# Four of ten turned x tiles change their copying engine, and a written order of pieces is revised

## The chip, the cores and the metric

The kernel runs on one core of a Trainium2 chip, as one program with one launch. The time is device microseconds of that core. Before the change the median of three runs is 315.41 us (315.05 to 315.96). TensorE multiplies matrices, VectorE and ScalarE do elementwise work, GpSimd does elementwise work and issues the loads, SyncE issues the stores. Each of them works through its own queue in order and waits for the others by semaphores.

## The reference

Two computations follow each other. The first is an attention over 8 batches of 8 heads with 576 positions of 64 values, where a position looks back at most 127 positions and a bias falls off linearly with the distance:

```
scores = scale * np.matmul(q, k.transpose(0, 1, 3, 2))
bias = slopes[:, None, None] * (-np.abs(rel).astype(np.float32))[None, :, :]
mask = (rel >= 0) & (rel < window)
scores = np.where(mask, scores + bias[None], -1000000000.0)
attn = np.exp(scores - max) ; attn = attn / (sum + 1e-09)
x = np.matmul(attn, v), rows (batch, position), columns (head, value)
```

The second is a two-layer network on these 4608 rows of 512 columns:

```
h = x @ w_in                      # 512 -> 2048
g = np.where(h > 0.0, h, np.exp(np.minimum(h, 0.0)) - 1.0)
out = g @ w_out                   # 2048 -> 512
```

Inputs and output are float32; the kernel multiplies in float16.

## The kernel before

Both parts run interleaved, so that TensorE always has matmuls of one part while the other waits. Attention works by batch and by blocks of 128 positions: four whole ones and one of 64 in each batch (i = 0 to 4). For a block, TensorE makes the scores, ScalarE exponentiates them into the tiles EX, and VectorE multiplies these with a table of bias and mask (`weigh`, line 234). TensorE multiplies with the values (`values`, `all_values`), and VectorE takes the reciprocal of the row sums and normalises the result into a tile xn of 128 rows and 512 columns.

The network needs x with columns on the partitions. `turn_x` transposes an xn tile on TensorE, four matmuls into one PSUM bank, and one instruction (line 287) then copies that bank into the buffer xT, as float16. Which engine copies is an argument of `turn_x`, called `copy`. In batches 2 to 7 the bank is always `sp[3]`, the second half of the PSUM pair `spb`, which the scores and the last block's values use too.

The hidden layer runs in 144 steps (`hidden`). A step multiplies a part of `w_in` with columns of xT into one PSUM bank of 512 columns. From step 18 on the two banks `hp0` and `hp1` alternate, so a step can begin only when the bank of the step two before it is free again. To free it takes three instructions in a row: an exponential on ScalarE (line 313) and a clamp on GpSimd (line 315), or, for steps in the set SOFT, a Relu and an exponential on ScalarE (lines 309 and 311); and then the ELU on VectorE (line 323), which reads the bank and writes g. Earlier steps use three or more banks.

The output layer, beyond its first 256 rows, is done by Strassen's scheme on blocks of 128 rows and 256 columns: sums and differences of g blocks on VectorE (`sums`, line 354), 896 single products on TensorE (`product`, line 393), copies out of PSUM on ScalarE (`keep`, lines 400 and 402), combinations on VectorE and the stores.

The order of all this is written out in the kernel. The kernel builds one list for each kind of piece: f and b, i, j for the first two batches' turns, biases, scores and exponentials; v, r, n for values, reciprocal and normalising; t for the transposes of an x tile and tA or tD for its copy; h for a hidden step, p and q for its two activations (or the activation and the clamp), e for its ELU; o for one product, u, s1 to s4, c1 to c3 and m for what belongs to the output; k, x, y, w for later scores, their exponentials and the weighing; d for the turning of q and k of later batches; l for loads; a and C for tables. The string `SCRIPT` then names the kinds one after the other, and each name emits the next piece of its list; `o4` emits four products. An engine's queue is thus the SCRIPT cut down to the pieces of that engine. Within a kind the order can't change. tA is the name of the copy list whatever engine does the copy.

PSUM is tracked by tile: an instruction that writes one half of the pair `spa` or `spb` waits for those that still read the other half.

Of the kernel before, what the change touches and what calls it, by code (L numbers as in the profile page):

```python
# [18 lines left out]
def kernel(  # L19
# [58 lines left out]
    sp = [t[:, i, :] for t in (spa, spb) for i in range(2)]  # L78
# [9 lines left out]
    s1 = one([128, 2 * H * 6 * D], F16, "s1")  # L88
# [62 lines left out]
    with tc.manual_schedule():  # L151
# [127 lines left out]
        def turn_x(b, i, copy, bank, c0=0):  # L279
            n = 128 if i < 4 else 64  # L280
            o = (b * S + 128 * i) % RING
            x = xnt.pop((b, i)).rearrange("p g h d -> p (g h d)")
            t = bank.bitcast(F16)[:, c0:c0 + 512].rearrange("p (c r) -> p c r", c=4)
            for c in range(4):
                nc.tensor.transpose(t[:, c, 0:n], x[0:n, 128 * c:128 * c + 128], ident[0:n, 0:n])  # L285
            yield
            copy(xT[:, :, o:o + n], t[:, :, 0:n])  # L287
# [239 lines left out]
        SOFT = {15 + 8 * n + d for n in range(2, 2 * NTB) for d in (0, 1, 2, 3, 4, 7)} | set(range(11, 19)) | {20, 22, 23} | set(range(16 * NTB - 10, 16 * NTB + 8))  # L527

        SCRIPT = """
            f f fD b fD f f fA b fD i C C C i j b C i j v v b r j n r j n t j tD v v r  # L530
            h r n n p t f tD q fA
            h e i f j f fD f fA b fD p b q i i l e j
            h b p
            h j q j l
            h e p v q p i r l n v j
            h r n q e t l p b e i q tD
            h j l e v p
            h r n q v p v e
            h q r
            h p a e q O p n q  # L540
            h r e l n t p O a tA e q v
            h l r e
            h l p a l q O p l e
            h q l
            h e p n l q O p e l
            h q l e t O l tA p a l
            h a q l a f p l f O1 fD l
            h fA O2 l e O p l s3 q O s1 l q e f l f e fA f fD l f O fA fA l a o1 i O1 i a l j o1 O2 o3 s2 o2 l o2 j o2 W o3 j o2 i u i W j v o2 c1 o1 v o1 r o2 r j o1 n i n j o2 W o2 u o1 t o1 s4 o1 tA o1 v o2 j r
            h W n v W p o1 i r
            h q j d n l e o1 v p o1 t W o1  # L550
            h q tA r u l e o2 p o1 v d o1 i r q n
            h j n l e o1 t p W o2
            h u q d tA l o1 e o1 p i d v j q
            h d l e o2 p o1 r o2 W o1
            h q n l e o1 v p o2 r o1 v n q u
            h r c2 l e v p t l n o3 tA r o2 s1 o2 q l k n e o1 x
            h s2 y o2 w
            h p w o4 u o2 s3 q v o3 p e t o3 q o1 c1 o1
            h tA e u o1 r o1 p
            h n q d o3 c3 p t o1 e o1 m tA o4 s4 o1 u k q d  # L560
            h x e o2 p o1 w o2
            h y q d l o1 e o2 u o2 p o2 w o3
            h q c2 l e v p d o1
            h l r q n l o1 e o1 p o1 t o1 l o1 s1 tA o5 q l s3 k u e l
            h x s2 o2 p
            h w u s4 q o4 p o1 e o4 y o2 c1 o3 c3 o1
            h q m w o1 e o1 v u p o2 r
            h n q d o2 p t o2 e o1 tA o3 u k d q
            h e x d o2 p o3 w o2 u
            h q y l e o4 p o1 w o1  # L570
            h q d o1 l v p e v l o1 c2 q o3 r o1 r
            h l e n l v p o3 r o1 n o1
            h q n s1 u o2 p o1 e t o2 tA o1 c3 o3 s2 q k m u
            h e x s3 o2 p o2 w
            h q c1 o1 y o1 e o8 p o1 w o1 t o1 q
            h u e tA o2 p o1 v o1
            h r q n u o1 s4 o1 p o1 t o2 e tA o1 q o4 u k l e
            h x d o2 p o1 w o4 y
            h q c2 l e o2 p o3 w o2 l
            h q u e l o2 p v s1 l  # L580
            h q r l n o2 p o2 e o2 k u s2 q
            h x e o1 c3 o2 p o2 m o2
            h q c1 y e o5 w o2 p o2
            h w q o2 e p t o2 v u s3 q o3 r
            h tA n u s4 o2 p o1 t e o2 tA o1 q o4 u k l e d
            h x c3 o1
            h p w y q s3 o4 l o1 e o2 p o4 c2 l o2 q
            h w l e o2 p v l s1 o1
            h q l r s2 u o1 e m o1 p o1 v o1 n v q o3
            h r r e o1 n o1 p o2 n o2  # L590
            h u d q c1 t o1 s4 o1 tA o4 e o1 p t o2 tA o1 q k u
            h e x d o1
            h p d q o4 p o1 e o4 y o1 q o1 w o2
            h u w u o2 p o1 e v o3 q o1 r
            h n l e o2 p t l o2 s1 o1 tA o4 q c2 k l u e
            h x l d o2 p
            h s2 l q l o3 p o1 e o4 y o2 w o1
            h q w o2 u o1 v e p o2 r o1 q
            h n c1 o2 e p t o3 tA o1 c3 o3 s3 q m k u e
            h x s4 o2 p o1 w o4 u o1  # L600
            h q y e o6
            h p w u q o1 v p l e o5 r q o1
            h n l e t o1 l o1 c3 tA o3 s3 o2 p l k c2 u q l d m
            h x l e o3 s1 l o1 p o3
            h w q y o1 e o7 p o1
            h w u s2 q v p c1 o2 e v q o4 r o1 r v e o1
            h u n
            h r p n n q o3 t o1 e o1 tA o5 p s4 o1 t u
            h d tA q k p e o1 x o1 q o1 d o3
            h e y w o4 p o2 w o1  # L610
            h u q l o1 e o1 p o2 v
            h q r l n o1 c2 o1 l p o1 t e o2 tA o2 s3 o1 l o1 u k q s1
            h l x e o1 c3 o1 p o2 s2
            h m u q w o2 p o1 e o4 y o2 c1 o5
            h q w o1 e v u p o2 r
            h n q d o2 p t o2 e o1 tA o4 q s4 k u e
            h x o1
            h p w y q o4 l o1 e o2 p o4 w u o1
            h q l e o1 v p c2 l
            h r q n l o2 d p o2 l o1 t o1 e o1 tA o1 l o4 u s1 o1 q k l s3 l o1 x o1 s2  # L620
            h e u o2 p o1 s4 o5 q w o3
            h y c1 e o3 p o1 w o2
            h q v e p o1 v c3 u o2 q r v m r o1 n
            h r n o2 n p o3 e o2 u t o1 d o1 tA o1
            h q t e o2 tA o2 p k q
            h x e o2 p o3
            h u c2 q y l o1 e o4 p o2 w o2 l o1
            h q w u l e o1 v p o2 r o2 l o1 n q
            h u e l t p o2 s1 o3 tA
            h s2 q o1 c3 k p e m o1 x o1 s3 o6 s4 o1  # L630
            h q c1 y e o5 w o1 p o3
            h w q u v e p o2 r o1 u o1
            h n q d t o2 tA o1 e o3 p k d u q
            h x e o2 p o2 w
            h y q o2 e o1 p o4 w o2 q o1
            h c2 u e v p o2 r
            h q n s3 o3 t s1 o2 tA o4 e o1 p k u s2 q o2 d
            h x e o2 p o2 c3 o3 c1 o1 m q o1
            h w y e o4 s4 o1 p o3
            h w q u v e p v r v r o2 n o1 u o3 q  # L640
            h r n n o1 e o1 p o1 t o2 tA
            h q u e t o2 tA o2 p k q
            h x e o2 p o2 c2 o3 w o1 q o3
            h y e o1 s1 o2 p o3 w
            h q u o1 e v p o3 r o1 u
            h n q s2 o1 t p o2 e o2 tA o3 c1 o1 q k s3
            h x e s4 o2 p o1
            h w u q c3 o3 p m o1 e o4 y o7
            h q w u e v o2 r o1 u
            h n p t q o2 tA o3 e o2 p k c2 q  # L650
            h x e o2 p o1 w o5 q o3
            h y e o1 s1 o2 p
            h w u q o1 s2 o1 v u p e o6 q r o1
            h c1 n o2 p o1 e o2 k q c3 s3 m o1 x
            h e o1 y o1 w o5 s4 o2 p
            h w u q o1 t o1 p o1 e o3 v u q o2
            h tA e r o2 p o1 n o3
            h u q e v p v o4 q
            h c2 r e o2 p o1 n o5 q
            h u e o2 p o2 r o1 s1 o3 q o1  # L660
            h n u e t p o1 s2 o5 q
            h tA e o2 p o2 c1 t s3
            h q e o2 p o3 s4 o2 tA o1
            h q c3 u m e o2 p o5
            h q u e o2 p o5
            h q u e o2 p o5
            h q c2 e o2 p o4 s1 o1
            h q u e o2 p o3 s2 o2
            h q e o2 p o3 s3 o3 q
            h u e o2 p o2 s4 o1  # L670
            h q c1 o1 e o1 p o6 q
            h u e o2 p o2 c3 o3
            h m q u e o2 p o5 s3 o1 q
            h u e o2 p o3 s1 o1 P q c2 s2 o2 U o1 e o4 P u s1 s2 c4 P c1 s4 P U P U P U c4 c2 Z
        """

# [11 lines left out]
        def parts(f, *kinds):  # L688
            for x in kinds:
                job(x, next, f, None)  # L690
# [87 lines left out]
        n = 2 * NTB - 1  # L778
# [50 lines left out]
```

## Time and profile before

| what | value |
|---|---|
| median of 3 runs | 315.41 us (315.05 to 315.96) |
| the profiled execution | 315.81 us |
| its span, first to last instruction | 314.0 us |
| granted TensorE clock | 0.999 |
| x tile copies on ScalarE (line 287) | 37, of which 34 from `spb` |
| x tile copies on VectorE (line 287) | 3 |
| ELU on VectorE (line 323), 128x512 from the banks hp | 138, mean 682 ns |
| clamp on GpSimd (line 315) | 44, mean 663 ns |

The page gives busy time by engine and the chain of work that ended last, followed back from the end. The timeline gives instructions in order of time: start, duration, engine, line, operation, tiles written <- tiles read, shape, count, and in brackets the idle time ahead of it and what ended that. A row of the copy line gives the count, and the shortest, median and longest duration in ns. Rows of idle time are read as: who ended the wait, microseconds, times.

### The profile page before, as it was taken

What the parts mean: (1) busy time and instruction counts of PE and PEld (TensorE: products, weight loads), DVE (VectorE), ACT (ScalarE), POOL (GpSimd) and SP (SyncE); (2) the same over time, 40 slices, a digit from 0 to 9 for tenths busy, and PEclk for the clock granted to TensorE, in tenths of its full rate; (3) what the DMA queues carried; (4) which work ended last, traced back from release to release, by engine and by line L of the source; (5) the groups of instructions that cost most, each with busy time, mean ns of one, the idle gap of its engine ahead of it and who ended that gap; (6) DMA issues with size and microseconds to landing.
All of it is one profiled execution on the core that took longest, in us unless ns stands there. A gap on an engine that the chain in (4) does not pass through costs nothing.

```text
span 314.0 us, 10000 instructions
## 1 busy us (share of the span) xinstructions
PE 306.1 (97%) x4198; PEld 262.3 (84%) x4198; DVE 257.0 (82%) x499; ACT 250.8 (80%) x452; POOL 109.3 (35%) x163
## 2 busy tenths in 40 slices
PE   8899999999999999999999999999999999999995
PEld 6688876889888889888888888888899888898884
DVE  5658698989999888898889897969988787876773
ACT  4576778869897989878978898879988888868871
POOL 8947857570616052424343152506000001010000
PEclk9999999999999999999999999999999999999999
DMA  9999999987794839290929091939100000000113
GB/s 103 192 194 206 198 160 196 117 83 88 88 114 43 121 53 114 21 161 4 128 55 177 5 135 16 155 60 109 39 35 35 35 33 35 35 37 34 46 58 102
DMA packets 81870, 28.44 MB, mean 91 GB/s; under 512 B 68896, under 2 KB 77728, under 8 KB 81824
## 3 DMA queue, kind: packets, MB, share of 16 engines
q0 software_dynamic: 75920, 18.36, 63.8%
q1 hardware_dynamic: 5760, 9.37, 8.3%
q8 instruction: 33, 0.54, 0.7%
q14 instruction: 13, 0.11, 0.1%
q10 hardware_dynamic: 144, 0.07, 0.1%
HBM read 36.70 MB, written 9.44 MB: 147 GB/s over the span
## 4 chain that ended last, share of the span: by engine, by line
PE 87%; POOL 3%; DVE 3%; DMA 2%; ACT 2%; issue 1%; POOLq 0%; DVEq 0%
PE hp L302 37%; PE op L393 14%; PE av L393 13%; PE spa L223 3%; PE spa L267 3%; DMA VP<-in_v_dram 2%; PE spb L285 2%; PE spb L393 2%; PE spb L302 1%; PE spb L246 1%; DVE g L323 1%; POOL e L315 1%; PE spb L223 1%; PE op L329 1%; PE spa L329 1%
## 5 line engine op out<-in xcount | busy, mean ns | idle before, releaser
L302 PE MATMUL hp<-xT,wi 128*128 128x256 f16 (+3 forms) x1488 | 143.6, 245 | 0.7 <-DVE g L323 0.4
L302 PEld LDWEIGHTS <-wi 128*128 128x128 f16 x1600 | 119.7, 98 | 15.8 <-issue 4.8
L323 DVE SCALAR_TENSOR_TENSOR g<-e,hp 128x512 f16<-128x512 f32 x138 | 94.1, 682 | 31.2 <-ACT e L311 15.5
L315 POOL TENSOR_SCALAR e<-e 128x512 f32<-128x512 f32 x44 | 29.2, 663 | 161.2 <-ACT e L313 158.5
L309 ACT ACTIVATE e<-hp 128x512 f32<-128x512 f32 x98 | 58.7, 599 | 21.5 <-PE hp L302 17.6
L311 ACT ACTIVATE e<-e 128x512 f32<-128x512 f32 x100 | 63.5, 636 | 1.9
L393 PEld LDWEIGHTS <-S 128*128 128x128 f16 x544 | 50.1, 98 | 6.5 <-issue 1.3
L393 PEld LDWEIGHTS <-g 128*128 128x128 f16 x400 | 37.3, 98 | 5.1 <-issue 1.1
L234 DVE TENSOR_TENSOR EX<-EX,TAB 128x1024 f16<-128x1024 f16 x48 | 32.8, 690 | 3.0 <-ACT EX L229 2.5
L115 POOL DMA_DIRECT2D VP<-in_v_dram x40 | 34.4, 870 | 1.4 <-DMA s<-in_k_dram 0.6
L313 ACT ACTIVATE e<-hp 128x512 f32<-128x512 f32 x40 | 24.0, 600 | 7.6 <-PE hp L302 6.9
L393 PE MATMUL op<-T,S 128*128 128x256 f16 x192 | 30.0, 273 | 0.0
L393 PE MATMUL av<-T,S 128*128 128x256 f16 x176 | 27.6, 273 | 0.0
L229 ACT ACTIVATE EX<-spa 128x1024 f16<-128x1024 f32 x24 | 24.6, 1026 | 1.9 <-PE spa L223 1.6
L229 ACT ACTIVATE EX<-spb 128x1024 f16<-128x1024 f32 x24 | 24.4, 1017 | 0.0
L354 DVE TENSOR_TENSOR S<-g 128x1024 f16<-128x1024 f16 (+2 forms) x35 | 22.9, 667 | 0.3 <-PE op L393 0.2
L287 ACT COPY xT<-spb 128x512 f16<-128x512 f16 (+1 forms) x34 | 18.2, 535 | 6.1 <-PE spb L285 5.7
L393 PE MATMUL op<-wo,g 128*128 128x256 f16 x128 | 20.2, 273 | 0.0
L393 PE MATMUL av<-wo,g 128*128 128x256 f16 x120 | 18.3, 273 | 0.0
L109 POOL DMA_DIRECT2D st<-in_k_dram x24 | 16.2, 685 | 3.0 <-DMA s<-in_q_dram 1.9
L275 DVE TENSOR_TENSOR xn<-spa,rden 128x512 f16<-128x512 f32 x24 | 16.5, 687 | 0.6
L109 POOL DMA_DIRECT2D st<-in_q_dram x24 | 15.9, 667 | 0.7 <-DMA VP<-in_v_dram 0.6
(137 smaller groups left out, 419.3 us busy)
## 6 DMA issues: line engine op xcount, KB each, us to landing
out_dram<-ob SPq DMA_DIRECT2D x32, 256.0 KB, 3.2
VP<-in_v_dram POOLq DMA_DIRECT2D x32, 128.0 KB, 5.9
st<-in_k_dram POOLq DMA_DIRECT2D x24, 144.0 KB, 4.5
st<-in_q_dram POOLq DMA_DIRECT2D x24, 144.0 KB, 5.9
wi<-in_moe_w_in_dram POOLq DMA_DIRECT2D x4, 512.0 KB, 11.6
wo<-in_moe_w_out_dram POOLq DMA_DIRECT2D x4, 512.0 KB, 9.7
out_dram<-ob SPq DMA_DIRECT2D x7, 128.0 KB, 1.7
VP<-in_v_dram POOLq DMA_DIRECT2D x8, 64.0 KB, 6.0
```

What stands on the lines that cost most here:

```text
L109: nc.gpsimd.dma_start(st[b][32 * g:32 * g + 32, w, :, :, :, :].rearrange("p h n j d -> p (h n) (j d)"), (q, k)[w][b, 2 * g:2 * g + 2, :, : ...
L115: nc.gpsimd.dma_start(VP[b % 2][0:p, n, :, 0:D], v[b, :, 128 * n:128 * n + p, :].rearrange("h p d -> p h d"))
L229: nc.scalar.activation(unit(b, u)[:, g:g + 2, :, :], (spa, spb)[g // 2].rearrange("p g (h c) -> p g h c", h=2), AF.Exp, scale=0.125)
L234: V.tensor_tensor(out=e, in0=e, in1=TAB[:, int(u == 3), 2 * gp:2 * gp + 2, :, :], op=ALU.mult)
L302: nc.tensor.matmul(p[:, l * w + u0:l * w + u1], w_in_sb[:, c, fc * 128:(fc + 1) * 128], xT[:, c, x0:x0 + u1 - u0], start=(c == 0), stop=(c ...
L309: nc.scalar.activation(e[:, 0:n], p[:, 0:n], AF.Relu, scale=-1.0)
L311: nc.scalar.activation(e[:, 0:n], e[:, 0:n], AF.Exp, scale=-1.0)
L313: nc.scalar.activation(e[:, 0:n], p[:, 0:n], AF.Exp)
L315: nc.gpsimd.tensor_scalar(out=e[:, 0:n], in0=e[:, 0:n], scalar1=1.0, scalar2=0.0, op0=ALU.min, op1=ALU.max)
L323: V.scalar_tensor_tensor(out=gs[t][:, f0:f0 + nf, c0:c0 + w], in0=sh(es.pop((t, c0, f0))), scalar=1.0, in1=sh(hps.pop((t, c0, f0))), op0=A ...
L354: V.tensor_tensor(out=o, in0=a, in1=b, op=op)
L393: nc.tensor.matmul(o, a[:, j, :], b[:, j, :], start=j == 0 and i in (1, 2, 5), stop=j == 7, skip_group_check=True)
```

## The change

In batches 2 to 7 the copies of blocks i = 1 and i = 3 go to VectorE, those of i = 0, 2 and 4 stay on ScalarE. These are 12 of 30 copies, each of 128 partitions and 512 elements. They stay in the list tA.

```
-            parts(turn_x(b, i, copies[0], sp[3]), "t", "tA")
+            parts(turn_x(b, i, copies[i % 2], sp[3]), "t", "tA")
```

(`copies` is `nc.scalar.copy, V.tensor_copy`.) With it, SCRIPT is written anew. It holds the same pieces, each kind as often as before, and many stand a little earlier or later against the hidden steps, mostly by one step, some by up to five. The beginning, a part of the middle and the end:

```
-            f f fD b fD f f fA b fD i C C C i j b C i j v v b r j n r j n t j tD v v r
-            h r n n p t f tD q fA
-            h e i f j f fD f fA b fD p b q i i l e j
+            f f fD b fD f f fA b fD i C C C i j b C i j v v b r j n r j n t j tD v v r f r n
+            h fA n t p i tD j q
+            h e f f fD f fA b fD p b q i i l e j
...
-            h q n d o2 p t o2 e o1 tA o3 u k d q
-            h e x d o2 p o3 w o2 u
-            h q y l e o4 p o1 w o1
-            h q d o1 l v p e v l o1 c2 q o3 r o1 r
+            h n d o2 p t o1 e o2 tA o2 k d q u e
+            h x d o2 p o1 w o2
+            h y q d l o2 e o1 u o2 p o2 w o3
+            h q c2 l e o2 p o1 v l s1 v q o1
...
-            h x c3 o1
-            h p w y q s3 o4 l o1 e o2 p o4 c2 l o2 q
+            h x l e o2 p o1 w o4 y
+            h q c2 l e o2 p o3 w l o3 q o2 c3 o1 l
...
             h u e o2 p o3 s1 o1 P q c2 s2 o2 U o1 e o4 P u s1 s2 c4 P c1 s4 P U P U P U c4 c2 Z
```

More of the change, by code (lines that the diff above doesn't have):

```diff
@@ L529 @@
         SCRIPT = """
-            f f fD b fD f f fA b fD i C C C i j b C i j v v b r j n r j n t j tD v v r
-            h r n n p t f tD q fA
-            h e i f j f fD f fA b fD p b q i i l e j
[L533 to L536, printed above, removed]
-            h j l e v p
[L538 to L568, printed above, removed]
-            h e x d o2 p o3 w o2 u
-            h q y l e o4 p o1 w o1
-            h q d o1 l v p e v l o1 c2 q o3 r o1 r
[L572 to L585, printed above, removed]
-            h x c3 o1
-            h p w y q s3 o4 l o1 e o2 p o4 c2 l o2 q
-            h w l e o2 p v l s1 o1
@@ L589 @@
[L589 to L644, printed above, removed]
+            f f fD b fD f f fA b fD i C C C i j b C i j v v b r j n r j n t j tD v v r f r n
+            h fA n t p i tD j q
+            h e f f fD f fA b fD p b q i i l e j
+            h j
+            h p b j q i p l e
@@ new lines @@
+            h j q v p v l r
+            h r n q n b e p l t e i q
+            h j l e v p
+            h tD r n q v p
+            h r e q v n p
+            h e q r t n p O e tA q
+            h l e
+            h p q v p
+            h l e O r p l n a q
+            h l e l t a O tA p a l
+            h q a q l O e p l e q O l a O1
+            h a O2 l e l f p f fD l q
+            h l e O l p s3
+            h q l fA e l f s1 l p f fA f fD f l O fA q l a O e l o1 i O1 a i j o1 O2 o1 l s2 o6 l j o2 W o3 j o1 i i fA W u v j o2 r o2 c1 v o2 r o1 j o1 n i n j o2 W o1 t o2 tA o1 s4 o3 v j W
@@ new lines @@
+            h r u W v p o3 n i q r o1 d
+            h j l n e o1 t p v W o1
+            h tA q d u r l e o1 v p o1 i r n u q
+            h j n l e o2 p t W o1
+            h tA q d l o1 e i p o1 d o1 j o1 q v d
+            h l e o1 r o1 p o1 W o2
+            h q n l o1 e v p o1 v r o2 c2 q
+            h u n l r e o2 p t l o1 n v tA o2 r o1 s1 q k l n o1 x
+            h e s3 y o1
+            h s2 u o1 w o1 p o4 w o2 q o1 t o1 p o2 e o2 v q o2 r
+            h c1 tA e u o2 n p o1
+            h c3 q d o1 m t p o1 e o3 tA o2 d o2 q k u e
@@ new lines @@
+            h x d s4 o1
+            h p w y q o4 l o1 e o2 u o2 p o2 w o1
+            h q c2 l v e p o2 r o2 q l
+            h n d l t s1 p o3 l o1 tA o2 e q o2 l k u c3 e
+            h x l m s2 o2 p o1 s3 o4 u o2 w q o1
+            h y e o3 s4 o2 p o4 c1
+            h q w u e o1 v p o2 r o1 q
+            h n d o2 p t o1 e o2 tA o2 k d q u e
+            h x d o2 p o1 w o2
+            h y q d l o2 e o1 u o2 p o2 w o3
+            h q c2 l e o2 p o1 v l s1 v q o1
+            h l r e l o1 r o1 p o1 n o2 v u
@@ new lines @@
+            h q r n n o2 e p o4 t u o2 q tA o2 s3 k e
+            h x s2 o2 p o1 w
+            h q c1 o2 y o1 e o6 c3 o2 p o1 w o1 m o1
+            h q u o1 e o1 p v t r o2 tA n o1
+            h u q s4 t e o2 tA o3 d o2 p k u q o1 x
+            h l e o2 w p o4
+            h y c2 q l e o2 p o4 w o2 l q
+            h e l o1 v p o1 l
+            h r q n l u o1 e o1 p o4 s1 k u q c3
+            h x e m o1 s3 o2 p o3 s2 o1
+            h q c1 y e o5 w o2 p o4 w
+            h u q t e p o2 v tA q o2 r o1
@@ new lines @@
+            h n u s4 o1 t o1 d o1 tA o5 p o1 e k u q s3
+            h x l e o2 p o1 w o4 y
+            h q c2 l e o2 p o3 w l o3 q o2 c3 o1 l
+            h e l v s1 p
+            h l s2 q o1 u r o1 e v p m o1 v n o2 q o2
+            h r r e o2 n p o3 n o1
+            h u d q t p o2 tA o2 e t o2 tA o1 c1 o1 q k u e
+            h x s4 o2 p o1 w o5 q d o1
+            h y e o3 d o2 p
+            h u w q o3 v e u o2 p o2 r o2 n
+            h q l e o1 t p o2 c2 o2 tA l o4 q k l u e
+            h x s1 l o2 p o2 s2 o3 l o1 q o2 w
@@ new lines @@
+            h l y e o3 d o1 p o1
+            h w q o1 v u e p o3 r o2 q n o1
+            h c1 t p o2 tA o2 e o2 q k s3 u
+            h x e c3 o2 p o2 w o1 m
+            h u s4 q o2 p e o5 y o1 q o3
+            h l u w o2 p o1 v e o1 q o1 r
+            h n l c2 o1 t l p e o4 tA o1 d o1 l o1 q k s3 l u
+            h x e l s1 o1 l o1 p o2 w o4 q o2 c3 o2
+            h y m e s2 o2 p o1
+            h w u q c1 o2 v p e v o1 q r o1 v r n o2
+            h e o1 r o1 p o1 n o1
+            h n q t u o1 p o1 tA o2 e o2 t o1 d o1 tA
@@ new lines @@
+            h u q s4 k p e o1 x o1 q d o3
+            h e y o1 w o2
+            h p w u q o2 p o3 l o1 e o1 v q o3 r
+            h l n c2 o1 t l e p o4 tA o1 d o2 l o1 u o1 k q s1 l
+            h x s3 s2 o2 p o2 e o3 u o2 q o1 w o1
+            h y e o2 c1 o2 p
+            h w q o3 p v e o1 q o1 r o2
+            h n e o1 t p o2 tA o1 u c3 k q s4 m
+            h x e o2 p o1 w
+            h u q y o2 l o1 e o4 p o2 w o3 u
+            h q s3 l e v p l o2 r o1
+            h c2 q l n o1 s1 o1 l p o2 t o1 e o1 tA o1 l o3 s2 o1 q o1 l k u e l o1 x o1 d
@@ new lines @@
+            h s4 u o1
+            h p w q o4 p o1 e o4 y o2 c3 o3 c1 o1 m
+            h q w u o1 e o1 p v v q r o2 r o2 n o3 v u n o3 r o1
+            h n e o2 d p t
+            h q tA t e o2 tA o2 p s3 k u q o1 x
+            h c3 e o2 w p o5 y
+            h c2 q l e o2 p o3 w o2 l
+            h q u e l o2 m p o1 v o1
+            h r q l n o1 e o1 p t l o3 s1 tA
+            h u s2 q o3 p o2 e o1 k q s4 o1
+            h x e c1 o2 p o1 w o4 y o1 d o1
+            h q w o4 u o1 v e p o1 u o1 r o2 q o1 n
@@ L645 @@
+            h e t p o2 tA o2 d k u q
+            h x e s3 o2 p o3 w
+            h y q o1 e o2 p o4 c2 o1 q o2 w
+            h e o1 v p o2 r o1 q
+            h n u s1 t o2 tA o2 s2 o3 p k e u q d o3 x
+            h e c3 o2 p o2 m c1 o3 w o1 q o1
+            h y e o3 s4 o2 p o3 w
+            h q u v e p v r v r o2 n o1 u o3 q
+            h r n n o1 e o1 p o1 t o2 u tA
+            h q e t o2 tA o2 p k q
+            h x e o2 p o1 w o5 q o1 c2 o1
+            h y e o2 s1 o2 p o3 w
             h q u o1 e v p o3 r o1 u
-            h n q s2 o1 t p o2 e o2 tA o3 c1 o1 q k s3
+            h n q s2 o1 t p o2 s3 o2 tA o3 e o1 q k c1
@@ L649 @@
             h q w u e v o2 r o1 u
[L650 to L673, printed above, removed]
+            h n p o1 q t p o2 tA o2 e o1 q k c2
+            h x e o2 p o1 w o4
+            h q y e o7 p o1 w
+            h u s1 q v p e o3 u o2 r o1 q o1 s2 o2
+            h n o1 e o1 p o3 c1 k q s3 o2 y c3 o1
+            h e m x o2 t o4 p o1 w o1
+            h u w q o2 p o1 e v o1 q s4 o4
+            h u e tA u s3 v p o1
+            h r n q o2 p o1 e o4 v q r o1 c2 o2
+            h e n o2 p o1 r o1 s1 o2
+            h q n e o2 p o3 t s2 u o2 q
+            h u e o2 p o2 c3 o3 tA o1 m q
+            h e o1 t p c1 o3
+            h q tA e o2 p o3 s4 o3 q
+            h u e o2 p o4
+            h q u e o2 p o6 q
+            h u e o2 p o2 s3 o3
+            h q c2 e o2 p o5
+            h q u e o2 p o3 s1 o3 q
+            h u e o2 p o2 s2 o3
+            h q e o2 p o3 c1 o2
+            h q e o2 p o3 c3 o2
+            h q m u e o2 p o3 s4 o1
+            h q u e o2 p o5 s3 o1 q
             h u e o2 p o3 s1 o1 P q c2 s2 o2 U o1 e o4 P u s1 s2 c4 P c1 s4 P U P U P U c4 c2 Z
```

## The prediction

> **What bounds the kernel now.** I read the page first: the shares of the engines, then the granted clock, then the chain that ended last.
>
> ```profile
> PE 306.1 (97%) x4198; PEld 262.3 (84%) x4198; DVE 257.0 (82%) x499; ACT 250.8 (80%) x452; POOL 109.3 (35%) x163
> ...
> PE 87%; POOL 3%; DVE 3%; DMA 2%; ACT 2%; issue 1%; POOLq 0%; DVEq 0%
> ...
> core 0: 314.0 us, clock 0.999
> ```
>
> TensorE carries 87% of the chain at full clock. It issues the same 4198 matmuls after the change, so an edit on VectorE and ScalarE can pay only through TensorE's stalls. The busy share hides those below about 0.16 us, because a 128x256 matmul is booked with 273 ns while the next one starts 0.109 us later. So I went through TensorE's timeline and noted each place where a matmul starts later than the one before it allows. Stalls around row-group changes (0.09 us each, at every score block) come back in any order. The others are few. From 66 to 300 us: 0.14 (84), 0.25 (98), 0.44 (132), 0.12 (146), 0.14 (170), 0.21 (181), 0.33 (197) and 0.12 us (228), together 1.75. From 46 to 66 us: 0.44, 0.35 and 0.44. From 20 to 46 us: 0.18 (30.5) and 0.28 (42). That is 3.44 us in all, the most that a better order could win there.
>
> Then the timeline around 132 us, all engines, cut to the rows that matter (start, duration, engine, line, tiles):
>
> ```profile
> 131.05 0.69 DVE L354 TENSOR_TENSOR S<-g 128x1024 f16<-128x1024 f16 x1
> ...
> 131.10 1.11 POOL L315 TENSOR_SCALAR e<-e 128x512 f32<-128x512 f32 x1 [1.65 <-ACT e L313]
> ...
> 132.24 0.69 DVE L323 SCALAR_TENSOR_TENSOR g<-e,hp 128x512 f16<-128x512 f32 x1 [0.51 <-POOL e L315]
> ...
> 132.98 0.38 PE L302 MATMUL hp<-xT,wi 128*128 128x256 f16 x2 [0.28 <-DVE g L323]
> ```
>
> The clamp on GpSimd lasts 1.11 us where its median is 0.61, with a two-input fp16 VectorE operation above it. VectorE's ELU and the next use of that PSUM bank are late by as much. The stalls at 84, 98 and 197 us follow clamps of 0.72, 0.80 and 1.00 us.
>
> **The change, part by part.** *1. The copies.* By the rows of the copy line:
>
> ```profile
> L287 ACT COPY xT<-spb x34: 352/583/623, 32.7 to 284.9; 128x512 f16<-128x512 f16 x26, 128x256 f16<-128x256 f16 x8
> ...
> L287 DVE COPY xT<-spb x1: 418/418/418, 25.5 to 25.5; 128x512 f16<-128x512 f16 x1
> ...
>   PE spb L285: 5.7, 10
> ```
>
> Twelve copies of 128x512 leave ScalarE: 12 x 0.583 = 7.0 us of 250.8. VectorE takes 12 x 0.42 = 5.0 us, by its one copy from the same bank, and goes from 257.0 to 262. Both lie beside TensorE's 306, so the direct cost is nothing while the ELU behind a copy stays off the path; the slow rival below prices that. In the other direction, an activation queued behind the copy comes earlier. At 225 us it shows:
>
> ```profile
> 225.34 0.58 ACT L287 COPY xT<-spb 128x512 f16<-128x512 f16 x1 [0.63 <-PE spb L285]
> ...
> 225.82 0.60 ACT L313 ACTIVATE e<-hp 128x512 f32<-128x512 f32 x1
> ```
>
> The exponential runs right behind the copy, and its bank is used again 0.12 us late (228 us). With the copy gone it can start up to 0.48 us sooner, so that stall goes.
>
> *A rule against it.* The VectorE copy at 25.52 us ran above a clamp on GpSimd (25.41, 0.63 us, against 0.61 alone), so a copy out of PSUM costs the clamp 0.02 us here. The Trainium skill (SBUF — State Buffer, "Who interferes with whom") says that a VectorE copy can take the port pair that it shares with GpSimd, and then one waits for the other. Its page VectorE: DVE Perf Modes ("Why PSUM operands drop a tier") takes that back for a PSUM source. By the first rule alone a clamp under a moved copy would wait about 0.4 us; by the row, nothing. I take the row.
>
> *2. The order at the start, up to 19 us.* The fifth turn piece of batch 0 (the second part of q) now stands ahead of the first hidden step, not behind the first turned x tile. Its transposes need a load issued by GpSimd at 5.68 us:
>
> ```profile
> s<-in_q_dram POOLq DMA_DIRECT2D x1, 128.0 KB, 8.0
> ...
> 13.01 0.41 PE L246 MATMUL op<-VP,EX 128*128 128x65 f16 x8
> ```
>
> I can't carry a wait below 13.68 (5.68 + 8.0): the values ahead of the piece are issued by 13.3, so TensorE stands still for about 0.4 us, and then turns for 0.4 us (0.44 in the row at 14.65, 0.33 of it issue) before the first hidden step, which started at 13.26 and now would at about 14.15. In return the scores that followed the second hidden step (0.33 us) and the turn (0.33) fill the waits at 14.1 and 14.9 us (0.19 and 0.31). So the second hidden step, at 15.23, comes near 16.1, and the pieces after it, without those scores between them, 0.5 us late. From there TensorE has no slack to absorb it. I take +0.5; ends: 0, if the landing is earlier, and +0.9, if nothing is won back.
>
> *3. The order from 20 to 46 us.* The stall at 30.5 us is a hidden step that waits for VectorE's normalisation from the same PSUM pair, which stood behind a 1024-wide subtraction; the normalisation now comes two hidden steps ahead. That at 42 us is a turn that waits for a ScalarE read of the same pair; the turn now comes a hidden step earlier, with another bank before it. I take -0.3 of the 0.46; ends: -0.46 and, since other pieces move here, +0.5.
>
> *4. From 46 to 66 us.* Products and reciprocals alternate on one PSUM pair, each waiting for the other. The reciprocal moves ahead of a 0.41 us combination, but the alternation stays. I take 0; ends -0.6 and +0.6.
>
> *5. From 66 to 300 us.* The cover of a hidden step is TensorE's work up to the next use of its bank, two steps on. I counted the products (0.109 us each) in both orders. At 98 us there are 15 for 13: 0.22 of the 0.25 covered. At 132 us 18 for 14: 0.44 of 0.44, and the subtraction above the clamp has moved. At 181 us two more (0.22 of 0.21), at 197 us two more (0.22 of 0.33), at 84 us five more (0.55 of 0.14). With 228 us of part 1, 1.49 becomes 0.14. The stalls at 146 and 170 us (0.26) I leave. Against this, at 228 us a 0.68 us subtraction now precedes the weighing that then falls on the clamp at 228.4: +0.2. Products are only moved, so other steps lose cover (at 208 us seven products, at 189 us six): I allow +0.4, a little over one stall of the present size. Together -1.35 + 0.6 = -0.75; ends: -1.5, and +1.6 by the rival.
>
> *6. Queues.* GpSimd's 113 instructions, its loads and clamps, stand in the same order as before, and so do SyncE's stores. No load is moved past another: 0. The last two hidden steps and all products after them are written alike: 0 for the tail from 303 us.
>
> **Sum**: 0.5 - 0.3 + 0 - 0.75 = -0.55 us. The profiled execution took 315.81 us (span 314.0 and 1.8 around it); that gives 315.26. It lies 0.40 above the median of the three runs, 315.41, so against the median the forecast is 314.86, say 314.9. Measurement of this kernel can tell about 0.3%, 0.95 us, from no change: the forecast lies inside.
>
> **Rivals.** *A. Slower: the copy holds up the ELU behind it.* VectorE works in order. ScalarE sat idle ahead of ten copies for 5.7 us, 0.57 each, because the transposes came late; VectorE would stand as long, and the ELU behind it with it. From the trace, between the end of the ELU that follows each of the twelve places and the matmul that reuses its bank lie 1.20, 0.69, 0.88, 0.97, 1.03, 0.44, 0.36, 0.63, 0.05, 0.81, 0.18 and 0.28 us. A delay of 0.59 (copy and 0.17 from TensorE) exceeds five of them, by 1.64 us in sum; one of 0.99 (copy and 0.57) exceeds ten, by 4.6. Between them 0.75 costs 2.6: 314.9 + 2.6 = 317.5. It decides from a delay of about 0.6 us a copy. For it: VectorE is at 9 tenths in most slices from 60 to 240 us. Against it: two to five products stand between turn and copy in the new order, 0.22 to 0.55 us, in which VectorE does other work. *B. Faster by more*: the start costs nothing, and all that I counted as new stalls is absent: 314.86 - 0.5 - 0.6 - 0.16 = 313.6. Against it: the landing time above. *C. It does nothing*: stalls go and return elsewhere, parts 3 and 5 cancel, and the start remains: 315.41 + 0.5 = 315.9.
>
> **Chances.** The forecast 0.36 (its own range 314.0 to 315.8), C 0.20, B 0.12, A 0.32. Below 314.46, 0.3% under the median, lie B and 0.22 of the forecast's: faster 0.34. Above 316.36 lies A but for its mildest 0.02, and 0.02 of C's: slower 0.32. The rest, 0.34, is no change. The range runs from 313.2, a little under B, to 317.2, nearly A's middle: about 2 in 10 stay outside.
>
> **What would show it.** In the changed profile: copies on line L287, 25 ScalarE and 15 VectorE, the latter near 0.42; the first hidden step near 14.15 in place of 13.26, with TensorE waiting for the load; no wait for the ELU at 98, 132 and 197 us; clamps over 0.7 us only where a fp16 pair operation lies above them. The forecast is wrong if VectorE's ELU shows more idle time ended by matmuls or transposes, or if the wait of hidden steps for VectorE grows beyond 1.75 us from 66 to 300 us.

## The result, and the profile after

The changed kernel takes 317.61 us (median of 6 runs, 316.98 to 319.01), the kernel before 315.52 us on the same chip (6 runs, 315.05 to 315.96). The ratio is 1.0071, with a 95% interval of 1.0047 to 1.0094: slower by 0.7%, where 314.9 us had been forecast and the range ended at 317.2. The profiled execution took 316.98 us, 1.17 more than the one of before.

The page of the changed kernel, the lines that answer to those shown of before:

```profile
PE 306.4 (97%) x4198; PEld 262.9 (83%) x4198; DVE 260.3 (83%) x511; ACT 245.8 (78%) x440; POOL 109.0 (35%) x163
...
PE 89%; DVE 6%; ACT 2%; issue 1%; POOL 0%; DVEq 0%; POOLq 0%; ACTq 0%
...
core 0: 315.1 us, clock 0.998
```

ScalarE is 5 us less busy and VectorE 3.3 us more. (Rows that overlap are counted once there; the durations by themselves fall by 7.2 us and rise by 5.2, as forecast.) TensorE has the same matmuls at the same clock. What is new stands in the chain: VectorE holds 6% of it in place of 3%. The copy line, by source, has the predicted count, 25 on ScalarE and 15 on VectorE (three lines of other tiles are left out), and the predicted 0.42 us:

```profile
L287 ACT COPY xT<-spb x22: 354/579/588, 31.1 to 285.0; 128x512 f16<-128x512 f16 x14, 128x256 f16<-128x256 f16 x8
...
L287 DVE COPY xT<-spb x13: 377/424/425, 27.1 to 282.6; 128x512 f16<-128x512 f16 x13
```

To see where the time went I took the start of each of the 144 hidden steps and subtracted its start in the profile of before. Call that the offset of a step. Steps are counted from 0, like the rows of SCRIPT, so step 2 opens row 3. Apart from the start of the kernel, which drifts from run to run, a profile repeats: two runs that share rows of SCRIPT have the same differences over them to about 0.05 us. For the changed kernel the offset is -0.58 us at step 2 (19 us), +1.18 at step 24 (65 us) and +1.09 at step 142 (300 us). So all of the loss arises between 19 and 66 us; after 66 us nothing is lost and almost nothing won.

The largest single stall is at 27 us. The timeline of the changed kernel there, all engines, rows left out (columns: start, duration, engine, line, operation, tiles, shape, count, idle time ahead and what ended it):

```profile
25.99 1.05 PE L302 MATMUL spb<-xT,wi 128*128 128x128 f16 x16
...
26.64 0.60 POOL L315 TENSOR_SCALAR e<-e 128x512 f32<-128x512 f32 x1 [0.22 <-ACT e L313]
...
27.08 0.42 DVE L287 COPY xT<-spb 128x512 f16<-128x512 f16 x1 [0.81 <-PE spb L302]
...
27.55 0.40 PE L246 MATMUL spb<-VP,EX 128*128 128x65 f16 x8 [0.51 <-DVE xT L287]
...
28.04 0.60 ACT L313 ACTIVATE e<-spb 128x512 f32<-128x512 f32 x1 [1.50 <-PE spb L246]
...
28.67 0.18 DVE L253 RECIPROCAL rden<-spb 128x4 f32<-128x4 f32 x1 [0.62 <-ACT e L313]
...
28.77 0.66 DVE L323 SCALAR_TENSOR_TENSOR g<-e,hp 128x512 f16<-128x512 f32 x1
```

In the kernel before, TensorE and VectorE did the same work without a wait:

```profile
25.52 0.42 DVE L287 COPY xT<-spb 128x512 f16<-128x512 f16 x1
...
26.65 1.05 PE L302 MATMUL spb<-xT,wi 128*128 128x128 f16 x16
...
27.54 0.41 PE L246 MATMUL spb<-VP,EX 128*128 128x65 f16 x8
```

The copy is `tD` of batch 0's third turned tile. Before, it closed row 6 of SCRIPT and ran at 25.52, ahead of hidden step 7 in row 8, which writes the other half of the pair `spb`. Now it stands in row 8, behind that hidden step. Its four transposes were done by 24.6 us, but the pair is tracked as one tile, so the copy waits for the matmuls that end at 27.04 (0.81 us). The values, which write `spb` again, wait for the copy (0.51); the exponential of the hidden step waits for the values (1.50); the reciprocal, now ahead of the ELU on VectorE, waits for the exponential (0.62), and the ELU behind it comes late for the next hidden step. TensorE stands still for 0.68 us at 26.8 and 0.55 at 28.9.

At 132 us the change did what was forecast. The timeline of the changed kernel:

```profile
130.10 0.67 DVE L354 TENSOR_TENSOR S<-g 128x1024 f16<-128x1024 f16 x1
...
130.17 1.08 POOL L315 TENSOR_SCALAR e<-e 128x512 f32<-128x512 f32 x1 [9.44 <-DVE g L323]
...
131.28 0.69 DVE L323 SCALAR_TENSOR_TENSOR g<-e,hp 128x512 f16<-128x512 f32 x1 [0.51 <-POOL e L315]
...
132.02 0.60 PE L302 MATMUL hp<-xT,wi 128*128 128x256 f16 x4
```

The clamp is still 1.08 us long under the subtraction, but four more products cover it: the next hidden step loses 0.08 us where it lost 0.44. Yet from 66 to 300 us the stalls sum to 1.48 us, against 1.75 before, and the forecast had them fall by 0.75. Gone are those at 98, 170 and 228 us; new are 0.24 at 140, 0.13 at 210 and three of 0.07 (174, 176, 187), and the one at 146 grew from 0.12 to 0.22. (Those at 140 and 210 us stand at turns, where 0.10 had been usual.)

That list leaves out the blocks of scores, as the prediction's did. To include them I took, for each two matmuls in a row, the distance of their starts beyond the usual one, which is the median for that line and shape in the profile of before, and summed this from step 24 to step 142. Outside turns and score blocks it falls by 0.80 us, slightly more than forecast. At the turns it rises by 0.21, and in the 24 score blocks by 0.50, which makes the -0.09 of the offset. Three blocks hold 0.47 of the 0.50, those at 95, 166 and 192 us: there the scores that go into `spb` start right behind the copy of a turned tile that still reads it. At 192 us it is a copy that had moved to VectorE; it ends at 192.18 and those scores start at 192.24, 0.25 us behind the ones into `spa`.

The windows view from 66 to 305 us shows the trade (columns: busy us and instructions of TensorE, its weight loads, VectorE, ScalarE, GpSimd, then clock, DMA share, GB/s):

```profile
66.00:305.00 239.00, 238.20 (x3065) 207.54 (x3065) 207.72 (x394) 198.38 (x357) 62.27 (x87) 1.00 0.52 70
```

TensorE was as busy in the same window before, 238.24 us.

### The profile page after: what moved, and what is told of

Its sections match the earlier page's. It is cut to its first block, busy times and chain, and to the rows that moved or that the text cites. A ratio compares the mean times of both kernels' runs of the same rounds, so it can differ in the third digit from the quotient of the medians.

```text
span 315.1 us, 9999 instructions
## 1 busy us (share of the span) xinstructions
PE 306.4 (97%) x4198; PEld 262.9 (83%) x4198; DVE 260.3 (83%) x511; ACT 245.8 (78%) x440; POOL 109.0 (35%) x163
## 4 chain that ended last, share of the span: by engine, by line
PE 89%; DVE 6%; ACT 2%; issue 1%; POOL 0%; DVEq 0%; POOLq 0%; ACTq 0%
PE hp L302 37%; PE op L393 15%; PE av L393 14%; PE spa L223 3%; PE spa L267 3%; PE spb L285 3%; PE spb L393 2%; DVE g L323 2%; PE spb L302 2%; PE op L438 2%; PE spb L246 1%; PE spb L223 1%; PE spa L329 1%; DVE xn L255 1%; DVE QT L142 1%
## 5 line engine op out<-in xcount | busy, mean ns | idle before, releaser
L309 ACT ACTIVATE e<-hp 128x512 f32<-128x512 f32 x98 | 58.6, 598 | 26.8 <-PE hp L302 22.1
L393 PE MATMUL av<-T,S 128*128 128x256 f16 x176 | 26.6, 273 | 0.0
L229 ACT ACTIVATE EX<-spa 128x1024 f16<-128x1024 f32 x24 | 24.6, 1023 | 2.4 <-PE spa L223 1.9
L354 DVE TENSOR_TENSOR S<-g 128x1024 f16<-128x1024 f16 (+2 forms) x35 | 23.6, 675 | 0.2
L223 PE MATMUL spa<-QT,KT 32*128 32x256 f16 (+2 forms) x240 | 15.7, 251 | 0.0
```

Source lines behind the costliest of these rows:

```text
L223: nc.tensor.matmul(sp[g][:, 256 * h2 + o:256 * h2 + o + n], kt_[b % 2][r, k0:k0 + 255:2], qt_[b % 2][r, c0:c0 + 2 * n - 1:2], start=dh == ...
L229: nc.scalar.activation(unit(b, u)[:, g:g + 2, :, :], (spa, spb)[g // 2].rearrange("p g (h c) -> p g h c", h=2), AF.Exp, scale=0.125)
L309: nc.scalar.activation(e[:, 0:n], p[:, 0:n], AF.Relu, scale=-1.0)
L393: nc.tensor.matmul(o, a[:, j, :], b[:, j, :], start=j == 0 and i in (1, 2, 5), stop=j == 7, skip_group_check=True)
```

## The experiments

Three theories stood at first. Theory 1: the loss is the new order before 66 us, that is, the copy that was moved behind the hidden step, an ELU behind a reciprocal, and a start that hangs on a load. Theory 2, the slow rival of the prediction: VectorE's copies hold up its other work, so the loss comes with `copies[i % 2]` from 66 us on. Theory 3: the new order after 66 us brings stalls of its own. Both orders have issued the same pieces at the end of row 2 and at the end of row 24 (before the step at 66 us), so there SCRIPT can be cut and the parts joined.

Offsets of hidden steps in the profiles (us against the kernel before), with the ratios; "cost" is the difference of two offsets before rounding. The profiles of e10 and e12 are left out, since the clock fell in their first 20 us (last section):

| kernel | step 2 | step 24 | cost, rows 3 to 24 | step 142 | cost, rows 25 on | ratio (95%) |
|---|---|---|---|---|---|---|
| changed | -0.58 | 1.18 | 1.76 | 1.09 | -0.09 | 1.0071 (1.0047 to 1.0094) |
| e1_early_old | -0.34 | -0.35 | -0.01 | -0.45 | -0.10 | 0.9995 (0.9973 to 1.0017) |
| e2_early_new | -0.47 | 1.28 | 1.75 | 1.28 | 0.00 | 1.0068 (1.0022 to 1.0115) |
| e3_copies_only | -0.63 | -0.63 | 0.00 | 0.06 | 0.69 | 1.0033 (1.0011 to 1.0055) |
| e4_order_only | 0.08 | 1.85 | 1.76 | 5.23 | 3.38 | 1.0174 (1.0134 to 1.0214) |
| e5_copy_back | 1.04 | 1.61 | 0.57 | 1.53 | -0.08 | 1.0049 (1.0025 to 1.0072) |
| e7_start_old | -0.80 | 0.95 | 1.75 | 0.90 | -0.06 | 1.0059 (1.0034 to 1.0084) |
| e8_start_old_copy_back | -0.17 | 0.41 | 0.58 | 0.34 | -0.07 | 1.0020 (0.9998 to 1.0041) |
| e11_bank_old | -0.09 | -1.22 | -1.13 | -1.26 | -0.04 | 0.9976 (0.9955 to 0.9996) |

### The order after 66 us, with the copies (e1_early_old)

```diff
 SCRIPT rows 0 to 24: as before
-            h q n l e o1 v p o2 r o1 v n q u
+            h q n l o1 e v p o1 v r o2 c2 q
...
-            parts(turn_x(b, i, copies[0], sp[3]), "t", "tA")
+            parts(turn_x(b, i, copies[i % 2], sp[3]), "t", "tA")
```

> The first 25 rows of the order (up to about 66 us, before any moved copy) are the old ones, the rest and the twelve copies on VectorE are the new ones. Theory 1 (the loss was made by the new order before 66 us: a late copy at 27 us, an ELU behind a reciprocal at 29 us, and a start that hangs on a load): about the time of the kernel before, 315.5, between 315.0 and 316.2. Theory 2 (rival A, the copies on VectorE hold up the ELUs behind them, after 66 us): the loss stays, 317.4. Theory 3 (the new order after 66 us brings other stalls): 317.4 too, with waits of TensorE that the kernel before has not.

315.37 us (12 runs) beside 315.54. With the old rows up to 24, the new order and the VectorE copies together cost nothing and win 0.10 us in the profile. The slow rival, as the cause of this loss, has fallen.

### The order up to 66 us, with ScalarE's copies (e2_early_new)

```diff
-            f f fD b fD f f fA b fD i C C C i j b C i j v v b r j n r j n t j tD v v r
+            f f fD b fD f f fA b fD i C C C i j b C i j v v b r j n r j n t j tD v v r f r n
...
 SCRIPT rows 25 on, and the copies: as before
```

> The reverse: the first 25 rows are the new ones, the rest is the old order, and all copies are on ScalarE. Theory 1: the whole loss, 317.3, with TensorE waiting 0.5 to 0.7 us at 27 and again at 29 us, and a wider spread of the runs than the kernel before has. Theories 2 and 3: 315.5.

317.64 us, as slow as the whole change, without one moved engine. The loss is in rows 0 to 24.

### The copies alone (e3_copies_only)

```diff
-            parts(turn_x(b, i, copies[0], sp[3]), "t", "tA")
+            parts(turn_x(b, i, copies[i % 2], sp[3]), "t", "tA")
```

> The old order throughout, with the twelve copies on VectorE. Theory 2: 317.5 or more, since the order is not made for it. Theory 1: 315.5 to 316.0; where it lies above 315.5, single ELUs late behind a copy.

316.40 us, 0.3% slower; in the profile 0.69 us. So VectorE's copies do cost something in the old order, but not where the rival had put it. The timeline of this kernel at 139 us:

```profile
138.99 0.67 DVE L354 TENSOR_TENSOR S<-g,S 128x1024 f16<-128x1024 f16 x1
...
139.58 0.41 DVE L287 COPY xT<-spb 128x512 f16<-128x512 f16 x1
...
140.04 0.27 PE L285 MATMUL spb<-ident,xn 64*128 64x64 f16 x4
```

The copy stands behind a sum on VectorE, and the turn of the next block, which goes into the same bank, waits for it: 0.23 us here and 0.27 at 175 us, where 0.10 is usual. Scores wait more. At 85 us the copy runs from 85.34 to 85.76, behind a subtraction on VectorE, and the scores into `spb` start at 85.81; that block takes 0.35 us more than before, and the one at 191 us 0.36. Together the four places take 1.0 us more than before, and other places win 0.3 back. It is TensorE's next user of the bank that is late; the waits for an ELU at 98, 132, 181 and 197 us have their old lengths.

### The new order without VectorE's copies (e4_order_only)

```diff
-            parts(turn_x(b, i, copies[i % 2], sp[3]), "t", "tA")
+            parts(turn_x(b, i, copies[0], sp[3]), "t", "tA")
```

> The whole new order with all copies on ScalarE. If the new order needs the copies on VectorE: 318.0 to 318.5, with exponentials late behind a copy. If the engine of the copies is of no matter: 317.6, as the changed kernel. If copies on VectorE hold up ELUs even in the new order: 317.0 or less.

321.54 us (the diff is against the changed kernel). Rows 25 on now cost 3.38 us. The waits of TensorE in this profile (us in total, times, longest), of which the changed kernel has none for the turn and 0.2 for the scores:

```profile
PE spb L223 <- ACT xT L287: 1.3, 4, 0.5
PE spb L285 <- ACT xT L287: 1.3, 3, 0.5
```

and its timeline at one of them:

```profile
213.37 0.57 ACT L287 COPY xT<-spb 128x512 f16<-128x512 f16 x1
...
213.99 0.27 PE L285 MATMUL spb<-ident,xn 64*128 64x64 f16 x4 [0.45 <-ACT xT L287]
```

The new order places the next turn close behind the copy, and counts on the faster one. So the same edit of one argument is worth +0.69 us in the old order and -3.4 in the new. The copies and the order can't be priced apart.

### The copy put back (e5_copy_back, e8_start_old_copy_back, e9_late_copy)

In e5, against the changed kernel, `tD` goes back to the end of row 6 and the ELU ahead of the reciprocal in row 9:

```diff
-            h r n q n b e p l t e i q
+            h r n q n b e p l t e i q tD
...
-            h tD r n q v p
-            h r e q v n p
+            h r n q v p
+            h e r q v n p
```

> The changed kernel with two pieces put back: the copy of the third x tile (tD) stands again behind the step before it, as in the kernel before, and the ELU of the seventh step ahead of the reciprocal that follows it. Theory 1: 1.0 to 1.2 us less than the changed kernel, 316.5, and no waits of TensorE at 27 and 29 us in the profile. Theories 2 and 3: 317.6.

317.26 us. The stalls at 27 and 29 us are gone and rows 3 to 24 cost 0.57 us in place of 1.76. But the median fell by 0.35 us only, less than the gain of 1.0 or more that had been expected. In the profile the start took back the rest; TensorE's row shows the load as the cause:

```profile
14.43 0.44 PE L137 MATMUL spb<-ident,s 64*64 64x64 f16 x16 [1.40 <-DMA s<-in_q_dram]
```

In the changed kernel's own profile that load was there at 11.99 us, here at 14.38. So e8 makes the same repair with the old start (rows 0 to 2 as before):

> The changed kernel with its first three rows as in the kernel before (the turn piece back behind the first hidden step) and with the two pieces of the run before put back. Theory 1 in its present form (start about 1.3 us at the median by the load, waits at 27 and 29 us for the rest): 315.4 to 315.9, and the runs lie closer together than those of the changed kernel. If something else in rows 3 to 24 costs time: 316.3 or more.

316.46 us, half a microsecond more than the upper figure expected: rows 3 to 24 still cost 0.58 us, so that my account of the loss lacked a part. The distances of matmul starts beyond the usual place it. From step 2 to step 17 (19 to 43 us), where both orders give TensorE the same work but for four matmuls, they sum to 1.42 us in the kernel before, 2.32 in the changed one and 1.14 in e8: with the two pieces back, the new order wins 0.28 us there. From step 17 to step 24 they sum to 3.03 us before and to 3.89 in both the changed kernel and e8, 0.86 more. Three waits are new in that stretch of the changed kernel:

```profile
46.27 0.44 PE L137 MATMUL spb<-ident,s 64*64 64x64 f16 x16 [0.16 <-DVE g L323]
...
49.21 0.39 PE L178 MATMUL hp<-QT,KT 64*128 64x256 f16 x4 [0.23 <-DVE g L323]
...
57.66 0.27 PE L393 MATMUL spb<-T,S 128*128 128x256 f16 x1 [0.19 <-DVE xn L255]
```

By the same measure they are 0.35, 0.44 and 0.40 us, where the kernel before has 0.12, 0.06 and 0.15 at such a change of pieces. The first two, a turn of q and scores, wait for an ELU that still reads their PSUM tile; the third is a product behind a normalisation. No run takes the three away one by one. In the kernel before, the scores at 48 us have no wait:

```profile
48.31 0.38 PE L178 MATMUL hp<-QT,KT 64*128 64x256 f16 x4
```

e9 is the other half of the test: the kernel before, with `tD` alone moved to row 8.

```diff
-            h r n q e t l p b e i q tD
+            h r n q e t l p b e i q
...
-            h r n q v p v e
+            h tD r n q v p v e
```

> The kernel before with only the copy of the third x tile put two rows down, where the changed kernel has it (the ELU stays). Theory 1: TensorE waits about 0.65 us at 27 us, because the copy waits for a hidden step that writes the other half of its PSUM pair and the values wait for the copy; 316.1 to 316.3. Without that coupling: 315.5.

Its median is 316.31 us beside 315.81, a ratio of 1.0006 (0.9987 to 1.0024), which can't be told from no change. The profile can tell more: the offset goes from +0.26 at step 2 to +1.05 at step 24, 0.79 us, and the same two waits are there:

```profile
28.00 0.42 DVE L287 COPY xT<-spb 128x512 f16<-128x512 f16 x1 [0.99 <-PE spb L302]
...
28.48 0.40 PE L246 MATMUL spb<-VP,EX 128*128 128x65 f16 x8 [0.52 <-DVE xT L287]
```

The stall of 0.68 is that of the changed kernel; the one behind it is 0.31, not 0.55. The copy by itself is thus worth about 0.8 us, and copy and reciprocal together 1.2 (1.76 less 0.57, and 1.75 less 0.58).

### The start (e6_start_new, e7_start_old)

e6 is the kernel before with rows 0 to 2 of the new order; e7 the changed kernel with rows 0 to 2 of the old one:

```diff
-            h r n n p t f tD q fA
+            h fA n t p i tD j q
...
```

> The kernel before with only its first three rows as in the changed kernel, copies on ScalarE. If the piece ahead of the first hidden step hangs on its load: 316.2 to 317.0 at the median, with a wider spread of runs, and the first hidden step in the profile begins 0.8 us after the load lands, whenever that is. If the start costs nothing: 315.5.

> The changed kernel with its first three rows as in the kernel before. If the start costs 0.3 us at a landing near 13.7 us and the rows 3 to 24 cost 1.8 us: 317.2, and 1.7 us between the first hidden steps and the step at 65 us in the profile, against the kernel before. If the start made the larger part: 316.5.

e6: 316.05 us beside 315.81, ratio 1.0003 (0.9977 to 1.0030), between the two times expected. e7: 317.87 (7 runs), ratio 1.0059; the old start doesn't take the loss away, as rows 3 to 24 cost 1.75 us with it. The wait itself is real. In e6:

```profile
13.73 0.44 PE L137 MATMUL spb<-ident,s 64*64 64x64 f16 x16 [1.09 <-DMA s<-in_q_dram]
...
14.10 1.07 PE L302 MATMUL hp<-xT,wi 128*128 128x128 f16 x16
```

The first hidden step starts 0.84 us late there; 0.5 of it is back by step 2, since the scores now fill a later wait, and 0.34 remains. But in the changed kernel's own profile it started at 13.19, 0.07 early. What decides is which of two loads lands when. By the trace's transfers, the old start hangs on a load of values, which landed between 11.50 and 13.61 us in the profiles, the new one on the piece of q, between 11.99 and 14.46. The old start's offset at step 2 is the landing of the values less 12.64, that of the profile of before (e1: 12.29 and -0.34). The new start's is the landing of q less 13.35 (e6: 13.68 and 0.34; e5: 14.38 and 1.04). Early landings win less than that (e7 with the values at 11.50, e2 and the changed kernel with q at 12.60 and 11.99). So the new start costs the distance of the two landings less 0.71 us. Over all profiles but that of e12 the distance is 1.02 us in the mean and 0.79 at the median: an estimate of 0.3 and 0.1 us, a little more for the early landings. The timed runs don't resolve that: e5 is 0.8 us slower than e8, which differs from it in the start alone, but the changed kernel is 0.3 us faster than e7, and e6 0.2 us slower than the kernel before.

### The stalls that both orders have at 46 to 66 us (e10_bank, e11_bank_old)

The first products of the output use `sp[3]`, a half of `spb`, which the values, normalising and reciprocals of the last blocks use as well. The two banks of the first column of outputs were exchanged, so that the values find `spb` free, and row 18 was fitted to that. Here against the kernel before (e11); e10 adds the same to e1:

```diff
-        XY = {1: (sp[3], op), 2: (op, av)}
+        XY = {1: (op, sp[3]), 2: (op, av)}
...
-            h fA O2 l e O p l s3 q O s1 l q e f l f e fA f fD l f O fA fA l a o1 i O1 i a l j o1 O2 o3 s2 ...
+            h fA O2 l e O p l s3 q O s1 l q e f l f e fA f fD l f O fA fA l a i O1 i a l j o2 O2 o3 s2 ...
```

> The kernel before with only that exchange of banks. The same gain, 314.3 to 314.8. Against e10 it tells what the new order after 66 us with the copies on VectorE is worth: by the profiles so far 0.1 us in favour of e10, by the prediction's fifth part 0.75.

> Old order for the first 25 rows, new order and copies on VectorE after that (as in e1), and the output products of the second block row change places: those that went to the PSUM pair of the values' bank now go to the other bank, and the reverse, with one product moved behind a store's copy. If the three waits at 51, 53 and 64 us (0.44, 0.35, 0.44 us) come from the sharing of that pair: 314.2 to 314.6, 1.0 us under the kernel before. If the waits only move: 315.4.

e11: 314.71 us beside 315.51, ratio 0.9976 (0.9955 to 0.9996). e10: 314.70, ratio 0.9967 (0.9944 to 0.9989). TensorE's waits in the changed kernel have these lines, the first of which was 0.5 and the second 0.2 before:

```profile
PE spb L393 <- DVE rden L253: 0.7, 2, 0.3
...
PE spb L393 <- DVE xn L255: 0.4, 2, 0.2
```

In e11 neither is among them; its two longest are

```profile
PE op L438 <- DVE T L444: 1.2, 1, 1.2
PE hp L285 <- DVE xn L255: 0.5, 2, 0.3
```

The stalls at 51, 53 and 64 us are gone, one of 0.29 at 48 is new, and the offset falls by 1.13 us. On this repair the new order after 66 us (e10) and the old one (e11) are equal in time, so the twelve copies and all that was written around them win nothing that the runs can show.

### Three more moves of pieces on the old order (e12_three_moves)

Against e11: the normalisation ahead of the sums in row 10, a turn piece one step later in rows 17 and 18, and a subtraction behind the clamp and the ELU in row 57 (the one shown at 131 us in the prediction):

```diff
-            h p a e q O p n q
+            h p n a e q O p q
...
-            h a q l a f p l f O1 fD l
-            h fA O2 l e O p l s3 q ...
+            h a q l a f p l O1 fD l
+            h f fA O2 l e O p l s3 q ...
...
-            h p w y q s3 o4 l o1 e o2 p o4 c2 l o2 q
+            h p w y q o4 l o1 e s3 o2 p o4 c2 l o2 q
```

> The kernel before with the exchange of banks, and three pieces moved: a normalisation ahead of the subtraction that it stood behind (30 us), the second turn piece of batch 1 behind the next hidden step (42 us), and at 131 us the subtraction on VectorE from above the clamp on GpSimd to behind the ELU. If a VectorE operation with two SBUF inputs above it is what stretches that clamp, it falls from 1.11 to about 0.62 us and the wait of 0.44 us goes; with the other two waits (0.18 and 0.28) 0.9 us less than the exchange of banks alone: 313.7 to 314.0. If the clamp is slow for another reason, the wait at 131 us stays.

314.42 us (12 runs), ratio 0.9934 (0.9905 to 0.9962). The runs of before beside it were higher than at other times (316.22), so the ratio flatters it; its median is 0.29 under that of e11, and its profile from step 2 on 0.25. It missed the 313.7 to 314.0 that had been expected. It has the lowest median here and beats both kernels; the runs don't separate it from e11. The timeline of e12 at 131 us:

```profile
131.25 0.61 POOL L315 TENSOR_SCALAR e<-e 128x512 f32<-128x512 f32 x1 [1.64 <-ACT e L313]
...
131.89 0.69 DVE L323 SCALAR_TENSOR_TENSOR g<-e,hp 128x512 f16<-128x512 f32 x1 [0.60 <-POOL e L315]
...
132.50 0.69 DVE L354 TENSOR_TENSOR S<-g 128x1024 f16<-128x1024 f16 x1
```

Without the subtraction above it the clamp takes 0.61 us; in e11 it took 1.11 in this place. That shows the cause of the 0.44 us wait, which is gone. Its worth is another matter: waits of 0.14 and 0.23 us appear at 134.0 and 134.4, behind the work that was moved, and only 0.04 is won. The two early moves won 0.21 of the 0.46 us that stood there.

## Why the prediction was wrong

*Part 3, the order from 20 to 46 us, is the first step that failed.* It took -0.3 us with an end at +0.5 for "other pieces move here". The -0.3 came (0.28 in e8's profile), but two pieces that were moved cost 1.2 us, so the part measured +0.9, beyond its end. I went through the stalls of the kernel before and asked of each whether it would go. I did not ask of each piece that was moved what now stands between it and the last user of its PSUM pair. The copy `tD` had passed a hidden step that writes the other half, and the rule that decides this, tracking by pair, stood in my own description of the kernel. e5 and e8 against e7 and the changed kernel show the 1.2, e9 shows 0.8 of it in the old order.

*Part 4, 46 to 66 us,* is the second. It took 0 and measured +0.9, beyond the end of +0.6. "The alternation stays" was true, and was no reason for a cost of nothing: the alternation got a further wait at 57 us, two new waits for an ELU came at 46 and 49 us, which the part didn't consider, and e11 shows that the alternation was worth 1.1 us in the kernel before. How the loss divides between parts 3 and 4 is read from the gaps in the profiles, not from a run of its own.

*Part 5, 66 to 300 us,* took -0.75 and measured -0.05 to -0.10 (e1, e7, the changed kernel). The reasons held in places: the waits at 98 and 228 us went and that at 132 fell to 0.08. At 225 us the exponential no longer follows the copy, by the timeline of the changed kernel:

```profile
226.30 0.60 ACT L313 ACTIVATE e<-hp 128x512 f32<-128x512 f32 x1 [0.72 <-PE hp L302]
...
226.53 0.42 DVE L287 COPY xT<-spb 128x512 f16<-128x512 f16 x1
```

The count of covering products was too high at 84, 181 and 197 us. It had 0.11 us remain there, and 0.13, 0.11 and 0.36 do, with 0.08 at 132: at 197 us VectorE's subtraction, 1.10 us long, makes the ELU late (its rows stand in the last section), so that more cover met a longer wait. Fewer stalls than allowed came up between other pieces, so that in all the places that the part had counted it was about right, 0.80 us won. What failed is what it left out: stalls at row-group changes "come back in any order". They didn't. The score blocks took 0.50 us more and the turns 0.21, at the copies of turned tiles above all.

*Part 2, the start,* took +0.5. The mechanism is shown: TensorE waits for that load by name in e5 and e6. Its size was read from one landing, 8.0 us after the issue; the same transfer took 6.3 us in the changed kernel's profile. The estimate is now 0.1 to 0.3, which no timed run confirms.

*Part 1* held: counts, 0.42 us a copy, the direct cost of nothing. Of the slow rival, the sign is shown in the old order (e3, 0.69 us) and the place was wrong, since the scores and turns that use the bank next wait, and not the ELU. In the new order VectorE's copy is needed (e4).

*The sum* of what was measured, 0.1 to 0.3 at the start, 0.9, 0.9 and -0.1, is 1.8 to 2.0 us; the medians differ by 2.09. The forecast of -0.55 came from credit for nearly every old stall, and from a cost of nothing for the pieces that had moved between them. The rival that ended slower came near the measured time with its 317.5 us by luck, for a reason that the runs refute.

## What to carry to other kernels

When an order of work is rewritten, follow each moved piece rather than each old stall: list what now lies between it and the last and next users of its buffer, by the unit in which the buffer is tracked. A stall that goes gives back less than its length, since the work that caused it lands on a neighbour; here 0.04 of 0.44 us and 0.21 of 0.46. Look also at the pieces that wait in every order, since they needn't wait equally long. And an engine swap and the order written for it have no separate prices here, +0.69 or -3.4 us: join the halves of both orders at points where they have done the same work, and measure each half.

## What the runs showed of the hardware

*Loads at the start drift.* The same 128 KB piece of q landed between 11.99 and 14.46 us in profiles whose remainder repeats to 0.05 us, and the load of values before it drifts too, over 2.1 us. An order that hangs on the one or the other load is a draw of some tenths of a microsecond, and comparisons of a few tenths need step offsets, not medians.

*The clock can fall at the start too.* In the profile of e10 the granted clock was 0.67 from 14 to 16 us and 0.74 from 16 to 20, in that of e12 0.53 and 0.81; from step 0 to step 2 each lost 1.13 us. In the profile of before it was 1.00 there.

*The second of two is held up.* In the changed kernel at 196 us the clamp came first, and VectorE's subtraction is the long one, 1.10 us where it takes 0.69:

```profile
196.33 0.73 POOL L315 TENSOR_SCALAR e<-e 128x512 f32<-128x512 f32 x1 [0.42 <-ACT e L313]
...
196.50 1.10 DVE L354 TENSOR_TENSOR S<-g 128x1024 f16<-128x1024 f16 x1
```

At 130 us the subtraction came first, and the clamp is the long one, 1.08. The Trainium skill (SBUF — State Buffer, "Who interferes with whom") says that a VectorE instruction with two inputs from SBUF contends with a GpSimd instruction that reads SBUF, calls the port pair that they share an exclusive lock, and lets issue order decide who blocks. The rows agree on who is held up, though the clamp that came first took 0.73 us and not 0.61. If the second waits for the whole of the first, the subtraction would have ended 0.69 us after the clamp's end at 197.06, at 197.75; it ended at 197.60, somewhat sooner. The copy out of PSUM at 27.08 us, beside a clamp at 26.64, lengthened neither: 0.42 and 0.60 us.
